# Windowed attention with a Swish feed-forward: wider loads, DMA transposes, an fp32 decay table, paired score tiles and an order fixed on three engines

## Chip, cores, metric

One core of one Trainium2 chip. The metric is the device time of one execution in microseconds (us). The profile adds a span (a few us shorter than the time) and the granted clock of the matmul engine. I write PE for TensorE, DVE for VectorE, ACT for ScalarE, POOL for GpSimd, and SP for the engine that issues loads.

## The reference

Batch 8, 8 heads, 576 tokens, head size 64. Each token attends to itself and the 127 before it, with an ALiBi bias; the result (4608 tokens x 512) goes through a feed-forward of width 2048 with a Swish of its own beta per column.

```python
scores = scale * np.matmul(q, k.transpose(0, 1, 3, 2))
rel = pos[:, None] - pos[None, :]
bias = slopes[:, None, None] * (-np.abs(rel))[None, :, :]
mask = (rel >= 0) & (rel < 128)
scores = np.where(mask, scores + bias[None], -1e9)
attn = softmax(scores)          # written out in the reference
x = (attn @ v) as (4608, 512)
h = x @ w_in
out = (h * (1.0 / (1.0 + np.exp(-beta * h)))) @ w_out
```

## The kernel before

The work of a batch is a list of steps: T (transpose q and k on PE), SC (scores sps, exp, mask, giving the probabilities pt), PV (pt times v gives pv, which DVE normalises into xn), X (transpose xn on PE into xt, and copy that into XT). They are packed between the steps of the feed-forward, HS (hps = W1 by XT) and OS (ops = gT by W2). Only PE's order is fixed by hand. First, the eight banks of PSUM, the memory in which this kernel's matmul results lie: two for hps, two for ops, one score tile of two banks, and two in `psum_t`, which pv and xt share. `merged(a, before)`: the pv steps of half a batch run among the scores of the next half.

```python
psum_h = ctx.enter_context(tc.tile_pool(name="psum_h", bufs=2, space=bass.MemoryType.PSUM))
psum_o = ctx.enter_context(tc.tile_pool(name="psum_o", bufs=2, space=bass.MemoryType.PSUM))
psum_s = ctx.enter_context(tc.tile_pool(name="psum_s", bufs=1, space=bass.MemoryType.PSUM))
psum_t = ctx.enter_context(tc.tile_pool(name="psum_t", bufs=2, space=bass.MemoryType.PSUM))
# ... (cut) in SC, after the score matmuls of one pair of heads:
for e in range(2):
    h = 2 * p + e
    for half, cols in ((0, slice(0, OWN[m])), (1, slice(OWN[m], 512))):
        nc.scalar.activation(out=pt[:, e, cols], in_=sps[:, e, cols], func=ACTF.Exp,
                             scale=qscale, bias=bias[:, half, h : h + 1])
nc.vector.tensor_tensor(out=pt[:], in0=pt[:], in1=masks[m][:], op=ALU.mult)   # bf16
# ... (cut) in PV, after the pv matmuls of four heads into one bank of psum_t:
nc.vector.reciprocal(out=zs[0:nq], in_=pv[0:nq, :, D : D + 1])
nc.vector.tensor_tensor(out=xn[0:nq, 4 * g : 4 * g + 4, :], in0=pv[0:nq, :, 0:D],
                        in1=zs[0:nq].broadcast_to([nq, 4, D]), op=ALU.mult)
# ... (cut) the order on PE:
for b in range(B):
    for m in range(2):
        a = [T(b, sb) for sb in ((0, 1, 2), (3, 4))[m]]         # shortened
        a += [SC(b, m, p) for p in range(NP)]                   # shortened
        att += merged(a, before)
        before = pvx(b, ((0, 1), (2, 3, 4))[m])
```

The softmax here doesn't subtract the row's maximum and nothing guards it: scores larger than these inputs give would overflow.

## Time and profile before

| | before |
|---|---|
| time, median of 2 runs | 376.41 us (375.89 to 376.93) |
| span, granted clock of the profiled run | 374.6 us, 0.9 or more in 39 of 40 slices |
| PE / DVE / ACT / POOL busy | 90 / 60 / 57 / 23% of the span |
| between 90 and 350 us: PE waiting for another engine | 0.6 us |

The lines behind this table stand in the prediction.

```profile
PE 80%; DMA 6%; DVE 4%; ACT 4%; SPq 4%; issue 1%; POOL 0%; ACTq 0%
```

Followed back from the last instruction, 80% of the time passes on PE and 4% on DVE.

### The profile page before, as it was taken

Reading aid. Unit: us, or ns where it says so; the run is one execution under the profiler, and the core shown is the slowest. Engines: PE = TensorE matmul, PEld = TensorE weight load, DVE = VectorE, ACT = ScalarE, POOL = GpSimd, SP = SyncE. Lnnn points to the kernel's source line nnn. Section 1 sums busy time; section 2 is a strip of 40 time slices with the busy share of each in tenths; the row PEclk is TensorE's granted clock in tenths of the full one; section 3 lists DMA queues with packets and bytes.
Section 4 is the critical chain, followed back from the end, with each engine's and each line's share of the span. In section 5 each row is a group of like instructions: output and inputs, shape, how many; then the busy total and the mean of one; then the engine's idle time right before and its main releaser. Section 6 shows DMA issues by size and latency. Waiting matters only on the chain.

```text
span 374.6 us, 6713 instructions
## 1 busy us (share of the span) xinstructions
PE 338.5 (90%) x2529; PEld 172.7 (46%) x2529; DVE 224.2 (60%) x473; ACT 214.4 (57%) x437; POOL 84.4 (23%) x151
## 2 busy tenths in 40 slices
PE   2367687788999999999999999999999999999995
PEld 1145334434454455445454545454545445544442
DVE  3266467777665677665666776776767755533400
ACT  1453359375745875585846694668566854445421
POOL 7570703453122213112033303320100000000000
PEclk9999999899999999999999999999999999999999
DMA  9999999999297898954138440000000010001012
GB/s 166 209 206 202 193 195 214 192 216 180 76 214 159 159 186 170 205 126 107 50 96 187 109 104 31 28 30 29 30 28 30 30 57 29 29 29 58 28 56 86
DMA packets 121985, 42.40 MB, mean 113 GB/s; under 512 B 113232, under 2 KB 117344, under 8 KB 121952
## 3 DMA queue, kind: packets, MB, share of 16 engines
q1 hardware_dynamic: 117728, 37.77, 47.9%
q0 software_dynamic: 4224, 4.19, 6.7%
q8 instruction: 20, 0.33, 0.4%
q14 instruction: 13, 0.11, 0.1%
HBM read 36.71 MB, written 9.44 MB: 123 GB/s over the span
## 4 chain that ended last, share of the span: by engine, by line
PE 80%; DMA 6%; DVE 4%; ACT 4%; SPq 4%; issue 1%; POOL 0%; ACTq 0%
PE ops L283 34%; PE hps L267 32%; PE sps L197 4%; DMA fst<-in_k_dram 4%; PE tps L171 4%; SPq L83 4%; ACT pt L207 3%; PE xt L249 2%; PE pv L233 2%; DVE gT L273 2%; PE pv L229 2%; DMA fst<-in_v_dram 1%; ACT sig L272 1%; DVE pt L211 1%; DVE qkT L176 1%
## 5 line engine op out<-in xcount | busy, mean ns | idle before, releaser
L272 ACT ACTIVATE sig<-hps,beta_h 128x512 bf16<-128x512 f32 x144 | 99.5, 692 | 98.4 <-PE hps L267 87.4
L267 PE MATMUL hps<-XT,W 128*128 128x512 bf16 x576 | 150.7, 385 | 3.6 <-DVE gT L273 3.0
L283 PE MATMUL ops<-W,gT 128*128 128x512 bf16 x576 | 144.9, 379 | 0.0
L273 DVE SCALAR_TENSOR_TENSOR gT<-sig,hps 128x512 bf16<-128x512 bf16 x144 | 98.3, 683 | 53.0 <-ACT sig L272 52.4
L207 ACT ACTIVATE pt<-sps,bias 128x256 bf16<-128x256 f32 (+2 forms) x256 | 100.4, 480 | 34.9 <-PE sps L197 34.6
L267 PEld LDWEIGHTS <-W 128*128 128x128 bf16 x576 | 51.1, 98 | 56.5 <-issue 10.9
L283 PEld LDWEIGHTS <-gT 128*128 128x128 bf16 x576 | 51.3, 98 | 52.2 <-issue 1.7
L211 DVE TENSOR_TENSOR pt<-pt,mask 128x1024 bf16<-128x1024 bf16 x64 | 46.1, 720 | 21.2 <-ACT pt L207 20.0
L96 POOL CAST bst<-fst 128x512 bf16<-128x512 f32 (+1 forms) x40 | 24.6, 615 | 108.8 <-issue 78.7
L197 PE MATMUL sps<-qkT 64*128 64x256 bf16 (+2 forms) x320 | 28.3, 271 | 14.1 <-ACT pt L207 13.1
L104 POOL CAST vs<-fst 128x512 bf16<-128x512 f32 (+1 forms) x40 | 26.1, 659 | 65.0 <-PE pv L233 38.1
L176 DVE COPY qkT<-tps 128x1024 bf16<-128x1024 bf16 (+1 forms) x40 | 25.5, 637 | 21.5 <-PE tps L171 21.3
L171 PE MATMUL tps<-ident,bst 128*128 128x128 bf16 x320 | 28.8, 240 | 7.8 <-POOL bst L96 4.3
L239 DVE TENSOR_TENSOR xn<-pv,zs 128x256 bf16<-128x256 f32 (+1 forms) x80 | 33.7, 422 | 2.6
L289 ACT ACTIVATE osb<-ops 128x512 f32<-128x512 f32 x36 | 21.6, 601 | 20.8 <-PE ops L283 20.8
L233 PE MATMUL pv<-vs,pt 128*128 128x65 bf16 x320 | 31.0, 200 | 2.5 <-DVE xn L239 1.5
L171 PEld LDWEIGHTS <-bst 128*128 128x128 bf16 x320 | 23.5, 107 | 17.3 <-POOL bst L96 4.9
L197 PEld LDWEIGHTS <-qkT 64*128 64x128 bf16 x320 | 12.4, 97 | 38.2 <-issue 35.1
L233 PEld LDWEIGHTS <-pt 128*128 128x128 bf16 x320 | 23.6, 102 | 13.7 <-issue 1.8
L97 POOL CAST bst<-fst 128x512 bf16<-128x512 f32 (+1 forms) x40 | 25.3, 634 | 9.3 <-DMA fst<-in_k_dram 9.2
L229 PE MATMUL pv<-vs,pt 128*128 128x65 bf16 x256 | 25.8, 200 | 1.8 <-DVE qkT L176 1.2
L229 PEld LDWEIGHTS <-pt 128*128 128x128 bf16 x256 | 21.3, 102 | 8.3 <-DVE xn L239 1.3
(26 smaller groups left out, 74.3 us busy)
## 6 DMA issues: line engine op xcount, KB each, us to landing
out_dram<-osb SPq DMA_DIRECT2D x36, 256.0 KB, 2.0
fst<-in_q_dram SPq DMA_DIRECT2D x32, 256.0 KB, 4.8
fst<-in_k_dram SPq DMA_DIRECT2D x32, 256.0 KB, 4.8
fst<-in_v_dram SPq DMA_DIRECT2D x32, 256.0 KB, 5.0
W<-in_moe_w_in_dram POOLq DMA_DIRECT2D x4, 512.0 KB, 11.5
W<-in_moe_w_out_dram POOLq DMA_DIRECT2D x4, 512.0 KB, 12.6
fst<-in_q_dram SPq DMA_DIRECT2D x8, 128.0 KB, 4.2
fst<-in_k_dram SPq DMA_DIRECT2D x8, 128.0 KB, 4.2
```

The lines of the kernel that those rows point to most:

```text
L171: nc.tensor.transpose(out=tps[:, i, p, :], in_=src[:, i, 2 * p : 2 * p + 2, :].rearrange("r h d -> r (h d)"), identity=ident[:],)
L176: nc.vector.tensor_copy(out=QK[b % 2][:, :, :, P * sb : P * sb + rows], in_=tps[:, :, :, 0:rows])
L197: nc.tensor.matmul(o, lhsT=qk[64 * e : 64 * e + 64, 1, p, P * kb : P * kb + P], rhs=qk[64 * e : 64 * e + 64, 0, p, P * kb : P * kb + nq], ...
L207: nc.scalar.activation(out=pt[:, e, cols], in_=sps[:, e, cols], func=ACTF.Exp, scale=qscale, bias=bias[:, half, h : h + 1],)
L211: nc.vector.tensor_tensor(out=pt[:], in0=pt[:], in1=masks[m][:], op=ALU.mult)
L229: nc.tensor.matmul(pv[:, hl, 0 : D + 1], lhsT=weights(b, qb - 1, h, 1), rhs=vs[:, qb - 1, h, 0 : D + 1], start=True, stop=False,)
L233: nc.tensor.matmul(pv[:, hl, 0 : D + 1], lhsT=weights(b, qb, h, 0), rhs=vs[:, qb, h, 0 : D + 1], start=qb == 0, stop=True,)
L239: nc.vector.tensor_tensor(out=xn[0:nq, 4 * g : 4 * g + 4, :], in0=pv[0:nq, :, 0:D], in1=zs[0:nq].broadcast_to([nq, 4, D]), op=ALU.mult,)
L267: nc.tensor.matmul(hps[:], lhsT=W1[:, c, bass.ts(j, P)], rhs=XT[:, c, c0 : c0 + TOKG], start=(c == 0), stop=(c == NDM - 1),)
L272: nc.scalar.activation(out=sig[:], in_=hps[:], func=ACTF.Tanh, scale=beta_h[:, j : j + 1])
L273: nc.vector.scalar_tensor_tensor(out=gts[g][:, j, :], in0=sig[:], scalar=1.0, in1=hps[:], op0=ALU.add, op1=ALU.mult)
L283: nc.tensor.matmul(ops_[:], lhsT=gT[:, j, i * P : i * P + P], rhs=W2[:, j, :], start=(j == 0), stop=(j == NFF - 1),)
```

## The change

The intent: let the loads run nearer line rate, take transposes off PE, make the exponentials fewer, and order all the issuing engines by hand.

1. Two tokens of q, k or v lie side by side on a partition, so that a row of a load has 512 B and not 256.
2. From batch 2 on, q and k are transposed by DMA (`DT`), from batch 3 on also the attention result (`X`), both issued by SP.
3. One exp per score tile without bias, into fp32; DVE multiplies it with an fp32 table that holds decay and mask.
4. Score tiles are made in pairs, which takes four PSUM banks; `psum_o` and `psum_t` give one each.
5. PE, SP and POOL in a fixed order (ACT and DVE too in the prologue).
6. Smaller: outputs issued by POOL in halves of 64 rows, v cast in quarters on POOL, 6 load buffers and not 16.

The diff, cut to its core (cuts are marked with `...`):

```diff
-    psum_o = ctx.enter_context(tc.tile_pool(name="psum_o", bufs=2, space=bass.MemoryType.PSUM))
-    psum_s = ctx.enter_context(tc.tile_pool(name="psum_s", bufs=1, space=bass.MemoryType.PSUM))
-    psum_t = ctx.enter_context(tc.tile_pool(name="psum_t", bufs=2, space=bass.MemoryType.PSUM))
+    psum_s = ctx.enter_context(tc.tile_pool(name="psum_s", bufs=2, space=bass.MemoryType.PSUM))
+    psum_o = ctx.enter_context(tc.tile_pool(name="psum_o", bufs=1, space=bass.MemoryType.PSUM))
+    psum_t = ctx.enter_context(tc.tile_pool(name="psum_t", bufs=1, space=bass.MemoryType.PSUM))
 ...
+    decay = const.tile([P, H, 3 * P], F32, name="decay")
 ...
+                r.append(nc.sync.dma_start(
+                    out=f[:, h0:h1].rearrange("p h c d -> p h (c d)"),
+                    in_=src[b, h0:h1, 256 * u : 256 * u + 256, :].rearrange(
+                        "h (p c) d -> p h (c d)", c=2),
+                ))
 ...
+                    nc.sync.dma_start(
+                        out=qk[:, :, at : at + 64],
+                        in_=src[64 * half : 64 * half + 64, c].rearrange("p i f -> p (i f)"),
+                        transpose=True,
+                    )
 ...
+            ex = ex_pool.tile([P, 2, 512], F32, name="ex", tag="ex")
+            nc.scalar.activation(
+                out=ex[:, :, 0:w], in_=sps[:, :, 0:w], func=ACTF.Exp, scale=qscale)
+            pt = pt_pool.tile([P, 2, 512], BF16, name="pt", tag="pt")
+            if m == 0:
+                nc.vector.tensor_tensor(
+                    out=pt[:, :, 0:w], in0=ex[:, :, 0:w], in1=decay[:, 2 * p : 2 * p + 2, :],
+                    op=ALU.mult)
 ...
+            for r0, r1, at in cuts:
+                nc.sync.dma_start(
+                    out=XT[:, :, at : at + r1 - r0], in_=xnv[r0:r1], transpose=True)
 ...
+            head = [A(0, 1), A(2, 3), pv(0, 0), pv(1, 0), Bm(0, 1), pv(0, 1), x(0), pv(1, 1),
+                    x(1), Bm(2, 3), pv(2, 0), pv(3, 0), C, pv(2, 1), x(2), pv(3, 1), x(3)]
+            tail = [pv(4, 0), pv(4, 1), x(4)]
 ...
+    with tc.manual_schedule(engines={ENG.PE, ENG.SP, ENG.Pool}):
```

`A(0, 1)` is the pair of score tiles 0 and 1 of the first half batch, `Bm` of the second, `C` the tile of the last 64 tokens, `pv(qb, g)` block qb of queries for head group g.

## The prediction

> **What bounds the kernel now.** I read the page's slices first, then the groups of instructions, then the timeline of the matmul engine (PE), then the DMA view of single stretches.
>
> ```profile
> PE   2367687788999999999999999999999999999995
> DVE  3266467777665677665666776776767755533400
> DMA  9999999999297898954138440000000010001012
> GB/s 166 209 206 202 193 195 214 192 216 180 76 214 159 159 186 170 205 126 107 50 96 187 109 104 31 28 30 29 30 28 30 30 57 29 29 29 58 28 56 86
> ```
>
> One slice is 374.6/40 = 9.4 us. There are two regimes: up to about 90 us DMA is saturated and PE is at 0.2 to 0.8; from 100 us PE is at 0.9 or more and DMA empties. So a gain can come from two places: fewer bytes-in-waiting early, and less PE work late. Where the early one ends:
>
> ```profile
> 42.44 1.87 PE L267 MATMUL hps<-XT,W 128*128 128x512 bf16 x4 [0.52 <-DVE XT L254]
> 80.19 1.89 PE L267 MATMUL hps<-XT,W 128*128 128x512 bf16 x8 [0.73 <-DVE gT L273]
> ```
>
> The first line is the first feed-forward matmul: 42 us pass before one can run. Counting hps matmuls in stretches of 5 us, 66 are done at 80 us, so token group 0 (64 of them) ends there: 42 to 80 us for 13.8 us of its own matmuls. What PE work costs is read from distances between starts in a stretch where PE never waits:
>
> ```profile
> 241.91 0.19 PE L229 MATMUL pv<-vs,pt 128*128 128x65 bf16 x1
> 242.16 1.03 PE L267 MATMUL hps<-XT,W 128*128 128x512 bf16 x4
> 243.11 0.39 PE L197 MATMUL sps<-qkT 64*128 64x256 bf16 x4
> 243.44 1.04 PE L283 MATMUL ops<-W,gT 128*128 128x512 bf16 x4
> 244.31 0.39 PE L249 MATMUL xt<-ident,xn 128*128 128x128 bf16 x4
> 244.53 1.03 PE L267 MATMUL hps<-XT,W 128*128 128x512 bf16 x4
> 248.64 0.61 PE L171 MATMUL tps<-ident,bst 128*128 128x128 bf16 x8
> 249.09 1.03 PE L267 MATMUL hps<-XT,W 128*128 128x512 bf16 x4
> ```
>
> Four 512-column matmuls take 244.31 - 243.44 = 0.87 us (0.216 each); eight transposes 0.45; four 0.22; eight pv matmuls 0.25; a score tile 0.33, and the four hps before it take 0.95 where 0.87 is usual, so 0.42 with the change of array shape. Per batch: T 5 x 0.45 = 2.25, X 5 x 0.22 = 1.1, scores 8 x 0.42 = 3.4, pv 72 x 0.031 = 2.25, together 9.0 us; 8 batches 72 us. Feed-forward: 1152 x 0.216 = 249 us. Sum 321 us; the span is 374.6, so 54 us are lost. After 80 us there remain 9/10 or so of the feed-forward (235 us) and 6.2 batches (56 us), 291 of the 294.6 us there: **almost all of the loss, some 50 us, lies before 80 us, and later PE alone sets the time.**
>
> **What the Trainium skill says.** (1) "DMA: Bandwidth & Descriptors", Specifications, gives 512 B or more as the least transfer for line rate. The trace agrees that 256 B is slow: between 3 and 12 us nothing but q, k, v moves, at 227 GB/s on average, whereas the weights in 24 to 34 us are written at
>
> ```profile
> q0 software_dynamic: 1644, 1.64, 97.1%
> ```
>
> 1.64 MB bf16, read as twice that in fp32, in 97% of 10 us: 340 GB/s read. (2) "VectorE: DVE Perf Modes", The TRN2 errata section, has (N+151)/0.96 ns for an fp32 add of two tensors, while bf16 pairs go at double rate. The present bf16 mask multiply of 1024 elements takes 690 ns on the timeline, (512+151)/0.96 = 691: agrees; no fp32 case is in this trace. (3) "ScalarE: Activation LUTs", What ACT_TABLE_LOAD costs, has 186 + 0.833 N ns with immediate operands. osb (N = 512): 612 against 601 in the groups; agrees. (4) The VectorE page, The three transpose paths, has 1309 ns for a 128x128 DMA transpose; no run here shows one.
>
> ```profile
> L289 ACT ACTIVATE osb<-ops 128x512 f32<-128x512 f32 x36 | 21.6, 601 | 20.8 <-PE ops L283 20.8
> L207 ACT ACTIVATE pt<-sps,bias 128x256 bf16<-128x256 f32 (+2 forms) x256 | 100.4, 480 | 34.9 <-PE sps L197 34.6
> L211 DVE TENSOR_TENSOR pt<-pt,mask 128x1024 bf16<-128x1024 bf16 x64 | 46.1, 720 | 21.2 <-ACT pt L207 20.0
> L171 PE MATMUL tps<-ident,bst 128*128 128x128 bf16 x320 | 28.8, 240 | 7.8 <-POOL bst L96 4.3
> L249 PE MATMUL xt<-ident,xn 128*128 128x128 bf16 x160 | 16.7, 231 | 0.0
> ```
>
> **The change, part by part.**
>
> *Rows of 512 B.* 256 B at 227 GB/s over 16 engines are 18 ns a row. If an engine's share of 435 GB/s gives 9.4 ns for the bytes, 9 ns are fixed; 512 B would then take 28 ns, 290 GB/s (an estimate from the page's fabric figure and the trace). The first group now waits for 512 tokens of q, k, v (3.1 MB, 11 us, landed near 14 us) and a first quarter of W1, not for 7.7 MB. What then bounds is batch 0's own chain: DVE has 4 x 0.96 + 4 x 1.22 us of multiplies, 4 copies of 0.69, 8 normalisations of 0.6, 4 copies of 0.42, some 18 us, starting near 7 us, and the scalar engine builds the decay table first. **First hps near 28 us instead of 42.**
>
> *Group 0* runs 9 HS alone (about 1.3 us each, bounded by the two hps banks, as two HS took 82.71 - 80.19 = 2.5 us before), then packs batch 1's attention into 7 HS. DVE there has 26 us. 12 + 26 to 28 gives 38 to 40 us, the 38 of before. End of group 0 near 66 to 68 us instead of 80: **-13 us.**
>
> *Transposes off PE.* T stays for batches 0 and 1, X for 0 to 2: PE loses 6 x 2.25 + 5 x 1.1 = 19 us, nearly all after 80 us, where PE is the bound: full worth. They become about 54 + 27 DMA transposes of 128 KB, issued a batch ahead, while the DMA row is at 0 to 4 from slice 18 on; hidden unless one takes over some 3 us. With the weights gone this leaves 36 us a batch for 12 us of loads and 9 to 14 transposes.
>
> *Scores in pairs.* Two tiles share one change of shape. The e = 0 and e = 1 matmuls run side by side (four of 256 took 0.33, not 0.43), so a first pair is 2 x (0.108 + 0.054) + 0.2 = 0.52, a second 0.63, the tail tile 0.44: 2.75 us a batch against 3.4. **-5 us.** PE work in all 321 - 19 - 5 = 297 us.
>
> *One exp per tile, fp32 table.* ACT: 768 and 1024 elements by the formula less the observed 10 ns, 0.82 and 1.03 us, per batch 4 x 0.82 + 5 x 1.03 = 8.4 us, against 100.4/8 = 12.6. DVE: 4 x 0.96 + 5 x 1.22 = 9.9 us a batch against 5.8, +33 us in all, against which 19 us of qkT copies and 10 us of XT copies go away. DVE stays near 228 us, but with a shorter span and its work shifted: in the late part per batch 9.9 + 10 x 0.6 + 18 x 0.68 = 28 of 36 us, 78%. Worth nothing directly, as neither engine is the bound there.
>
> *PSUM.* Score pairs take four banks, so ops and the shared bank for pv and xt fall from two buffers to one. A pv tile's bank comes free after about 0.2 + 0.18 + 0.42 + 0.2 = 1.0 us plus any wait for DVE, and an item between two pv is 0.87 us. Three or four pairs of pv a batch follow each other directly: 0.5 us each, about 2 us a batch. ops: 36 turns, an HS and a step between them (1.2 us) against 0.2 + 0.6 + the wait for ACT. I put both at **+14 us** in all (my choice in 5 to 25), and at the end three turns without an HS between them **+3 us**.
>
> *POOL.* Casts of v in quarter pieces and outputs issued there: about 12 us of casts and 9 issues of up to 0.8 us (the W issues took that) per batch, under 36 us.
>
> Sum: end of group 0 at 67, then 291 - 23 = 268 us of PE, stalls 14, end 3: 352 us. A fixed order worked out for three engines should pack group 0 better than I could and put the pv steps apart, so I take **343 us**.
>
> **Rivals.**
> 1. *PSUM and DVE become the bound.* The trace speaks for it a little: late in the run PE idle is 0 only because every bank had a second one. With 1.2 us multiplies in front of each gT and reciprocal the stall could be 1 us at each of 80 pv tiles and 36 ops turns: +50 instead of +14 us over 24 us gained on PE: 370 us or more, "same".
> 2. *DMA transposes are slow or hold up loads.* SP issues loads and transposes in one order, and a transpose waits for casts. If one takes 4 us, 14 x 4 + 12 = 68 us a batch against 36: the run becomes DMA bound late, 400 us and more. Against it: the DMA row shows free time for it, and two batches keep T on PE as if to cover the loaded start.
> 3. *No stall at all.* The order hides both: 62 + 268 + 3 = 333, or with a group 0 near 30 us long, 325 us.
>
> **Range and chances.** From 3 (325) to my sum with stalls at 25 (363): 322 to 362. Faster by over 2% means under 369: only a good part of rival 1 or 2 prevents it: 0.90; same 0.07; slower 0.03.
>
> **What would show it.** Right: first hps near 28 us; group 0 done at 62 to 68; DMA above 270 GB/s while q, k, v load; exp rows at 0.82 and 1.03 us, multiplies at 0.96 and 1.22; PE at 0.9 in late slices with idle in front of pv and ops of 10 to 20 us, released by DVE xn and ACT osb. Wrong: waits of sps for DMA (rival 2), hps waiting for gT late (rival 1), GB/s unchanged near 220, or POOL casts so delayed that transposes come late.

## The result, and the profile after

The changed kernel takes **421.69 us** (419.70 to 423.67, 2 runs), against 376.41. Every ratio below is the mean time of one kernel's fast runs over the mean of the kernel before's fast runs in the same rounds, so it isn't quite the ratio of the medians quoted. Here it is 1.121, 95% interval 1.108 to 1.134: 12% slower. The profiled run: span 417.7 us, granted clock 0.961.

From the page after: PE's busy tenths and its granted clock in 40 slices of 10.4 us, then the last chain by engine and by line.

```profile
PE   3448675679679788589948974799998999999984
PEclk9999969799899999899989998799999999999999
...
PE 51%; DVE 25%; ACT 9%; DMA 5%; issue 4%; SPq 3%; another core or an unknown queue 1%; POOL 1%; ACTq 0%
PE hps L399 22%; PE ops L416 21%; DVE pt L313 8%; ACT ex L302 6%; DVE pt L306 5%; DVE gT L405 5%; PE pv L360 4%; DMA XT<-xn 4%; DVE xn L366 3%; PE sps L282 2%; ACT sig L404 2%; SPq L264 2%; DVE qkT L243 1%; DMA fst<-in_k_dram 1%
```

The wall of nines that stood from slice 11 to the end now starts only at slice 27; before that PE falls to 4 and 5 again and again. PE's work did shrink (324.3 us busy against 338.5). DVE went from 4% of the chain to 25%, though its busy time hardly rose (232.1 us against 224.2) and its share of the span fell from 60% to 56%. The new multiplies (L313 and L306) alone are 13% of the chain, 54 us of 418. So DVE isn't full. It is *in the way*. What PE waited for in the whole span (total us, times, longest):

```profile
PE pv L360 <- DVE xn L366: 21.1, 18, 3.1
PE hps L399 <- DMA XT<-xn: 19.3, 5, 6.5
PE xt L380 <- DVE xn L366: 9.1, 7, 3.7
PE sps L282 <- DVE qkT L243: 8.4, 6, 2.5
```

And the new operations themselves, groups by form (busy us, then mean ns of one):

```profile
L313 DVE TENSOR_TENSOR pt<-ex,decay 128x1024 bf16<-128x1024 f32 x32 | 40.9, 1320 | 13.3 <-ACT ex L302 13.3
L306 DVE TENSOR_TENSOR pt<-ex,decay 128x768 bf16<-128x768 f32 x32 | 31.6, 1027 | 9.6 <-ACT ex L302 9.5
L302 ACT ACTIVATE ex<-sps 128x1024 f32<-128x1024 f32 x32 | 30.9, 1021 | 18.4 <-PE sps L282 18.4
```

How one wait of each of the two big kinds comes about is seen in the timeline after (start, us, engine, line, operation):

```profile
155.86 0.62 PE L282 MATMUL sps<-qkT 64*128 64x128 bf16 x12
...
157.28 0.41 PE L360 MATMUL pv<-vs,pt 128*128 128x65 bf16 x8
...
157.60 2.36 DVE L313 TENSOR_TENSOR pt<-ex,decay 128x1024 bf16<-128x1024 f32 x2 [0.22 <-ACT ex L302]
...
159.88 0.18 DVE L365 RECIPROCAL zs<-pv 128x4 f32<-128x4 f32 x1
...
160.54 0.42 DVE L366 TENSOR_TENSOR xn<-pv,zs 128x256 bf16<-128x256 f32 x1
...
161.02 0.42 PE L360 MATMUL pv<-vs,pt 128*128 128x65 bf16 x8 [1.60 <-DVE xn L366]
...
164.64 5.19 SPq L264 DMA_TRANSPOSE qkT<-bst  x4
...
165.32 0.42 DVE L366 TENSOR_TENSOR xn<-pv,zs 128x256 bf16<-128x256 f32 x1
...
169.94 1.27 SPq L386 DMA_TRANSPOSE XT<-xn  x1
...
174.18 1.87 PE L399 MATMUL hps<-XT,W 128*128 128x512 bf16 x4 [5.14 <-DMA XT<-xn]
```

The first six lines: a pair of score tiles at 155.86 leads to two multiplies back to back on DVE, 2.36 us. A pv that PE finished at 157.69 needs DVE for a reciprocal of 0.18 and a product of 0.42 us, but stands behind both (the product also behind one gT). It gives its bank back at 160.96, 3.3 us after PE was done with it. There is one such bank now, so the next pv waits, and in PE's fixed order everything behind it waits too. Neither pv needs these two multiplies: their own probabilities were multiplied at 150.37. In the whole list of PE's waits there is no line of pv for pt (there is one for pc, the probabilities of the last 64 tokens, 4.5 us).

The last four: xn is ready at 165.74, but SP has begun to issue four transposes of q and k for the next batch, 1.3 us each. The transpose of xn is issued at 169.94, and the next feed-forward matmul starts at 174.18, 8.4 us after xn. This wait comes from SP's order, not from a late xn. Then the four matmuls take 1.87 us where 1.03 is usual: the Trainium skill ("TensorE: Matmul & The Clock Gate", Part 1) says that PE falls to half rate after an idle window of some 3.4 us, and here PE had been idle for 5.14. The granted clock agrees: 0.91 between 160 and 180 us, 1.00 before and after. Waits here cost something twice.

### The profile page after: what moved, and what is told of

It is laid out like the page before. It is cut to its first block, busy times and chain, and to the rows that moved or that the text cites. A ratio compares the mean times of both kernels' runs of the same rounds, so it can differ in the third digit from the quotient of the medians.

```text
span 417.7 us, 6134 instructions
## 1 busy us (share of the span) xinstructions
PE 324.3 (78%) x2276; PEld 154.7 (37%) x2317; DVE 232.1 (56%) x413; ACT 187.7 (45%) x274; POOL 139.8 (33%) x212
## 4 chain that ended last, share of the span: by engine, by line
PE 51%; DVE 25%; ACT 9%; DMA 5%; issue 4%; SPq 3%; another core or an unknown queue 1%; POOL 1%; ACTq 0%
PE hps L399 22%; PE ops L416 21%; DVE pt L313 8%; ACT ex L302 6%; DVE pt L306 5%; DVE gT L405 5%; PE pv L360 4%; DMA XT<-xn 4%; DVE xn L366 3%; PE sps L282 2%; ACT sig L404 2%; SPq L264 2%; DVE qkT L243 1%; DMA fst<-in_k_dram 1%
## 5 line engine op out<-in xcount | busy, mean ns | idle before, releaser
L399 PE MATMUL hps<-XT,W 128*128 128x512 bf16 x559 | 153.2, 395 | 24.5 <-DMA XT<-xn 19.3
L432 POOL DMA_DIRECT2D out_dram<-osb x64 | 33.4, 527 | 199.8 <-ACT osb L422 199.8
L302 ACT ACTIVATE ex<-sps 128x768 f32<-128x768 f32 (+1 forms) x64 | 55.3, 915 | 29.9 <-PE sps L282 29.5
L313 DVE TENSOR_TENSOR pt<-ex,decay 128x1024 bf16<-128x1024 f32 x32 | 40.9, 1320 | 13.3 <-ACT ex L302 13.3
L204 POOL CAST vs<-fst 64x512 bf16<-64x512 f32 x60 | 44.9, 748 | 7.2 <-DMA fst<-in_v_dram 4.8
L192 POOL CAST bst<-fst 128x1024 bf16<-128x1024 f32 (+1 forms) x36 | 35.4, 1004 | 24.2 <-PE tps L239 9.1
L360 PE MATMUL pv<-vs,pt 128*128 128x65 bf16 x448 | 26.4, 204 | 20.3 <-DVE xn L366 15.6
L306 DVE TENSOR_TENSOR pt<-ex,decay 128x768 bf16<-128x768 f32 x32 | 31.6, 1027 | 9.6 <-ACT ex L302 9.5
L360 PEld LDWEIGHTS <-pt 128*128 128x128 bf16 x448 | 22.4, 105 | 37.9 <-DVE xn L366 23.0
L282 PE MATMUL sps<-qkT 64*128 64x128 bf16 (+1 forms) x320 | 20.7, 262 | 9.2 <-DVE qkT L243 8.4
L365 DVE RECIPROCAL zs<-pv 128x4 f32<-128x4 f32 (+1 forms) x80 | 14.1, 176 | 14.7 <-PE pv L360 14.7
```

Source lines behind the costliest of these rows:

```text
L192: return eng.tensor_copy(out=o, in_=f[:, h0:h1].rearrange("p h c d -> p c h d"))
L204: r = e.copy(out=o, in_=a) if e is nc.scalar else e.tensor_copy(out=o, in_=a)
L282: nc.tensor.matmul(o, lhsT=qk[64 * e : 64 * e + 64, 1, p, P * kb : P * kb + P], rhs=qk[64 * e : 64 * e + 64, 0, p, q0 : q0 + n], start=Tru ...
L302: nc.scalar.activation(out=ex[:, :, 0:w], in_=sps[:, :, 0:w], func=ACTF.Exp, scale=qscale)
L306: nc.vector.tensor_tensor(out=pt[:, :, 0:w], in0=ex[:, :, 0:w], in1=decay[:, 2 * p : 2 * p + 2, :], op=ALU.mult)
L313: nc.vector.tensor_tensor(out=pt[:].rearrange("p e (n w) -> p e n w", n=2), in0=ex[:].rearrange("p e (n w) -> p e n w", n=2), in1=d, op=AL ...
```

## The experiments

Three theories, after the first reading:

- **XT late.** The DMA transposes of X come late behind those of q and k in SP's order; put X back on PE and most of the loss goes.
- **Load.** The fp32 multiplies bring DVE to its limit; whatever the order, the time stays.
- **Placement.** PE's fixed order puts pv just behind scores, with one bank for pv and xt. A DVE instruction of 1.3 us is then on PE's path, while with more distance and two banks it would cost little. (I first took these scores to be pv's own; the lists show that they are not, see point 5 of the change.)

All ratios: below 1 is faster than the kernel before. The medians are of all 4 runs, the ratios of the fast ones alone: one run of `e1` and two of `e12` were slow.

**1. Undo one thing at a time** (before in these rounds: 375.18 us).

X back on PE:
```diff
-    PE_X = 3
+    PE_X = 8
```

> After, with the X transposes of all batches back on PE (PE_X 3 to 8), all else the same. Theory A (X by DMA arrives late, because the DMA transposes of X stand in the SP order behind four 1.26 us transposes of qkT and the loads): the 19.3 us that hps waits for DMA XT<-xn go, and with them most of the low-clock stretches after those stalls (granted clock 0.91, 0.91, 0.86 at 160, 200, 260 us, some 8 us); PE gets 25 X steps of 0.22 us back (5.5 us): about 421 - 27 + 6 = 400 us. Theory B (one bank for pv and xt, freed only after fp32 multiplies on DVE): the stalls of hps go but the X steps queue up for the same bank, each with a wait of up to 1 us for DVE: 415 us or no gain at all.

Measured: 425.93 us, 1.127 [1.118, 1.136]. No gain. The wait of hps for XT is gone from its waits, but xt waits for DVE xn 27.1 us now (9.1 in the change) and pv for xn 21.3. XT late is not the cause *by itself*: remove it and PE stands at the next place, at xt, which in PE's order follows directly behind the pv whose xn it needs.

Tables and exp tile in bf16:
```diff
-    decay = const.tile([P, H, 3 * P], F32, name="decay")
+    decay = const.tile([P, H, 3 * P], BF16, name="decay")
```
(and the same for `decayt` and `ex`)

> After, with ex and both decay tables in bf16, so that the multiply can run at double rate: 1024 elements in about 0.7 us for 1.32, 768 in about 0.55 for 1.03 (the old bf16 mask multiply of 1024 took 0.69). DVE loses some 36 of 83 us of multiplies. Theory B (pv waits for DVE xn, which stands behind pairs of multiplies): PE waits for DVE xn, pc and qkT (some 24 us late, 20 us early) fall by a third to a half: 400 to 410 us. Theory A alone: XT is late all the same, 415 to 420 us.

Measured: 383.51 us, 1.023 [1.018, 1.028]: 38 us, most of the loss. The multiplies fall to 743 and 621 ns. Waits of PE in this kernel:

```profile
PE hps L399 <- DMA XT<-xn: 15.1, 3, 5.7
PE pv L360 <- DVE xn L366: 6.9, 10, 1.9
```

That fits load *and* placement, as it makes the instruction both cheaper and quicker. It takes later runs to tell them apart.

PSUM divided as before the change, score tiles one at a time (pairs need four banks, so the two go together):
```diff
-  psum_s bufs=2   psum_o bufs=1   psum_t bufs=1      # shortened
+  psum_s bufs=1   psum_o bufs=2   psum_t bufs=2
-        A = lambda *ps: (None, lambda: SC(b, 0, ps))
+        A = lambda *ps: (None, [(None, lambda p=p: SC(b, 0, (p,))) for p in ps])
```

> After, with the PSUM banks shared out as before (score tiles 1 of two banks, ops 2, pv and xt 2) and score tiles one by one, each a step of its own, everything else as after. Theory B: PE waits for DVE xn (21 us for pv, 9 for xt) and for ACT osb (4) mostly go, 0.1 us a score tile comes back for changes of shape (6 us): 395 to 405 us. If pairs of score tiles matter more than banks: 420 us or more. Theory A: hps still waits about 19 us for XT.

Measured: 401.84 us, 1.070 [1.065, 1.076]: 20 us back. The wait of pv for xn is gone, that of hps for XT stays, and those of xt for xn and of sps for the exp have grown (9.1 and 0.7 us in the change):

```profile
PE hps L403 <- DMA XT<-xn: 18.6, 3, 7.2
PE xt L384 <- DVE xn L370: 11.1, 11, 2.4
PE sps L282 <- ACT ex L306: 10.6, 20, 1.2
```

Rows of 256 B, two DMAs where the change has one:
```diff
-                    in_=src[b, h0:h1, 256 * u : 256 * u + 256, :].rearrange(
-                        "h (p c) d -> p h (c d)", c=2),
+                        in_=src[b, h0:h1, 256 * u : 256 * u + 256, :].rearrange(
+                            "h (p c) d -> p c h d", c=2)[:, c],     # for c in range(2)
```

> After, with q, k and v fetched in rows of 256 B again (one DMA for even and one for odd rows; same places in memory), all else the same. q, k, v then move at about 220 GB/s instead of 286 in the first 10 us: first hps some 4 to 5 us later; group 0 to 2 some 5 to 10 us later, nothing later on unless the DMA transposes collide with loads: 427 to 435 us. If the loads are hidden (rival): 421 us.

Measured: 424.34 us, 1.131 [1.126, 1.136]. The 512 B rows are worth about 1% here, which is within the noise. They do run faster: between 3 and 10 us the changed kernel moves 286 GB/s, this run 222. But the first hps comes at 36.4 us here and at 35.6 in the change.

**2. Combinations** (before: 375.29). I put pv half a batch behind its scores, as it was before the change (`e6`, and `e8` with bf16 and X on PE). Both gave **wrong results**, relative error 0.10: the loads of the next batch cast v into a buffer that pv of two batches back still had to read. An order is also a claim on buffers; the later pv needs a third buffer for v. I draw nothing from their times (432.67 and 395.47 us).

> After, fp32 table and all, with one thing changed in PE's order for batches 2 to 7: the pv and X steps of a half batch stand beside the score steps of the next half, as in the kernel before, and not one or two items behind their own score steps. Theory C (the fp32 multiplies hurt as latency: PE's fixed order puts pv so close behind its scores that exp, two multiplies and the bank's release lie on PE's path): PE waits for DVE fall by more than half, and most of what bf16 gave (38 us) comes back: 385 to 400 us. Theory D (the fp32 multiplies hurt as load: DVE has too much to do in each group): no gain, 412 to 425 us.

> bf16 tables, X on PE and the later pv order together. If distance and length of the multiplies are the same wait (theory C), the order adds little to bf16: within 5 us of the bf16 version with X on PE. If DVE load matters beside it, 8 us or more.

`e7` joins the edits of `e1` and `e3` (`PE_X = 8`, bf16 tables and exp tile), `e9` those of `e1`, `e3` and `e4`:

> The bf16 version with all X transposes on PE as well. The bf16 version alone took 383 us and still has 15.1 us in which hps waits for DMA XT<-xn, in 3 stalls, and 0.97 mean clock. Theory A in its weaker form (late XT is real, but with fp32 multiplies in front the X steps on PE waited just as long for DVE): now X on PE should pay: 383 - 15 - 5 for the clock + 6 for 100 transposes, 368 to 374 us. If X on PE still gains nothing, the waiting is for xn itself: 380 to 388 us.

> bf16 tables, X on PE, and the banks of before (score tiles singly in 1 buffer, ops 2, pv and xt 2). On the fp32 version the banks gave 20 us. If that was the wait for pv's bank behind fp32 multiplies, bf16 has taken most of it and 0 to 5 us are left, against 5 us for changes of shape and waits of sps for exp: 366 to 376 us. If the banks act on their own, 355 to 362 us.

Measured: `e7` 375.95 us, 1.002 [0.996, 1.008]; `e9` 381.20 us, 1.015 [1.007, 1.022]. Once the multiplies are short, X on PE is worth 2% where it was worth nothing in `e1`, and the second bank with single tiles alone is worth nothing (1.3 points worse). The parts don't add; each hides behind another.

**3. Distance with three v buffers** (before: 376.36). The edit, shortened: the head and tail lists of batches 2 and on are replaced by

```python
head = merged(scores_of_first_half,  pv_and_x_of_last_second_half) \
     + merged(scores_of_second_half, pv_and_x_of_own_first_half)
VS = [... for i in range(3)]     # and to make room: ptp 9, osb 3, sig 2 buffers
```

The order alone, all else as in the change (fp32, one bank, X by DMA):

> The earlier try of this order was wrong in its result and of no use: v of batch b+1 was cast into the buffer that pv of batch b-1 still read. Here v has three buffers (ptp 9, osb 3, sig 2 to make room); the order of pv one half batch behind the scores, fp32 table kept. Theory C (latency of exp, multiplies and bank between a score step and its pv): 385 to 400 us. Theory D (DVE load): no gain, 412 to 430 us.

Measured: 408.89 us, 1.077 [1.067, 1.088], so 4 points better than the change. Its profiled run was slow, so of its waits I take only the kinds:

```profile
PE pv L361 <- DVE xn L367: 28.1, 15, 3.1
PE hps L400 <- DMA XT<-xn: 2.5, 1, 2.5
```

pv still waits for its bank, hps for XT hardly. This is the opposite of `e4`, where the banks took away the first wait and left the second. The result fell between load and placement, and settled nothing between these two.

Order with bf16 and X on PE, one bank; then with two banks and single tiles ("the repaired kernel"; its lists place the single tiles and X a little differently, see 5); then bf16 with q and k, not X, transposed on PE:
```diff
-    PE_T = 2
+    PE_T = 8        # and DT returns at once for these batches
```

> The same order with three v buffers, bf16 tables and X on PE; without the order it took 376 us. Theory C: 365 to 378 us, the order and bf16 heal the same wait. If one bank for pv and xt is now the wait, it stays at 370 to 380 us.

> All the repairs at once, so near the kernel before in its attention: banks of before, score tiles singly, pv half a batch behind, X one or two steps behind its pv, bf16 tables, X on PE; kept of the change: 512 B rows, T by DMA, one exp a tile, the fixed order. PE work is then 249 + 8 x (3.4 + 2.25 + 1.1) + 4.5, some 307 us, and first hps at 36 us. If the order and the banks are what is left: 340 to 355 us, faster than both. If the early part still decides: 362 to 370 us.

> bf16 tables, all T on PE, X of batches 3 to 7 still by DMA: no transposes of qkT stand in front of XT in the SP order. Theory A (queue): hps waits for DMA XT fall from 15.1 us to under 5 us. If it is the transpose's own 2.7 us to landing: they stay at 10 us or more. PE gets 6 x 2.25 = 13.5 us of T, and T uses the one bank: 385 to 397 us in all.

Measured: `e13` 379.48 us, 1.009 [1.004, 1.014]. `e15` **366.73 us, 0.975 [0.969, 0.980]**, the first to beat the kernel before. Order alone (1.009 against 1.002 of `e7`) and banks alone (1.015) each gave nothing to this version, both together almost 3 points. `e14` 398.83 us, 1.059 [1.052, 1.066]: without the q and k transposes in SP's order the wait for XT is gone, so it was the queue; but pv now waits 11.3 us for the copies of q and k on DVE, as their tile shares the one bank.

**4. The split between the theories** (before: 374.70). In the repaired kernel I put single parts of the change back.

fp32 again, and its control: bf16 with the same smaller buffers that fp32 needs to fit.
```diff
-    decay = const.tile([P, H, 3 * P], BF16, name="decay")     # decayt and ex too
+    decay = const.tile([P, H, 3 * P], F32, name="decay")
-  ptp bufs=10   osb bufs=4   sig bufs=3      # shortened; e19 has these three alone
+  ptp bufs=9    osb bufs=3   sig bufs=2
```

> The repaired kernel (366.7 us) with the fp32 decay table, fp32 exp tile and fp32 multiply put back, nothing else but one buffer fewer of three small tiles so that it fits. Latency theory (the long multiplies only hurt because they stand just in front of the pv matmuls and of the one pv and xt bank): with pv half a batch later and two banks it stays within 2% of the repaired kernel, 366 to 374 us, multiplies still at 1.03 and 1.32 us. Load theory (27 us more work on DVE overfill it, whatever the order): 385 to 410 us, with waits of pv and xt for DVE xn of 15 us or more.

> Control for the fp32 run: the repaired kernel, still in bf16, with the same smaller numbers of buffers for pt, osb and sig (9, 3, 2). Expected within 1% of the repaired kernel, 365 to 371 us; if it is 375 or more, the fp32 run can't be read as the cost of fp32.

Measured: `e16` 372.81 us, 0.995 [0.988, 1.001]; control `e19` 365.77 us, 0.974 [0.969, 0.979]. fp32 costs **2.1 points, 7 us**, where it cost 38 us in the change. The groups of `e16` by form: L318, the 1024-element multiply, has a median of 1225 ns, the 1226 ns of the change. Same instructions, same number, a fifth of the cost. With X on PE on both sides, as here, the change's order and bank make fp32 dearer still: `e7` to `e1` is 12.5 points, about 50 us. The load theory is out as the main cause.

X by DMA again (`PE_X = 3` instead of 8), and 256 B rows (the edit of `e5`):

> The repaired kernel with X of batches 3 and on made by DMA transposes on SP's queue, as in the change. If the wait of hps for XT seen after the change (19 us) comes from SP's order and not from the slow multiplies, it is here again at 10 us or more and the time is 374 to 385 us. If it came from xn being late behind the multiplies, it stays under 4 us and the time is 361 to 368 us, as PE does 5 us less work.

> The repaired kernel with q, k and v read in 256 B rows, two DMAs where there was one. In the change itself the rows were worth at most 1% because the early stretch waited for DVE and ACT. If the early stretch of the repaired kernel is bound by the same chain, 367 to 372 us; if the 512 B rows are what it lives on, first hps several us later and 376 us or more.

Measured: `e17` **360.18 us, 0.960 [0.950, 0.969]**, best of all; the wait for XT doesn't come back, so the DMA transposes of X are a gain of some 1.4 points (5 to 6 us) in the repaired kernel. This is small: the intervals touch, and two of the four runs of `e17` had a clock of 0.995 (358 us), two of 0.981 (362 us), where the control at 0.979 to 0.984 took 365 to 366. `e18` 365.37 us, 0.972 [0.967, 0.978]: no loss from 256 B rows here either. PE's busy tenths and the last chain in `e17`:

```profile
PE   1555865768999999999999999999999999999994
...
PE 81%; DVE 9%; ACT 5%; issue 2%; DMA 1%; SPq 0%; POOL 0%; ACTq 0%
```

**5. The missing corner** (before: 374.83). Order and banks put back together: the buffers of `e12`, the bank edit of `e4`, and the lists of `e15`. These are not quite the lists of `e12`: single score tiles are spread among the pv steps, the pv of one block follow each other, and X stands 3 to 6 steps behind its last pv, where in `e12` and in the change it follows directly. Nothing else is undone: fp32, X and T by DMA, 512 B rows and the fixing of three engines all stay.

> The change as it is (fp32 table, fp32 multiply, X and T by DMA, 512 B rows) with only the place of pv (half a batch behind its scores, X one or two steps later, three v buffers) and the PSUM division (two pv and xt banks, two ops banks, two single-pair score buffers) put back. Placement theory: order and banks together give back what neither gave alone (order alone 408.9, banks alone 401.8), 360 to 372 us, waits of hps for XT under 5 us. Load theory, or SP's order: 380 us or more, with pv waiting for DVE xn or hps for XT 10 us or more.

Measured: **368.46 us, 0.981 [0.976, 0.987]**. Its waits of PE between 81 and 330 us, the largest three:

```profile
PE pv L365 <- DVE pc L337: 1.3, 1, 1.3
PE hps L404 <- DVE gT L410: 1.0, 2, 0.6
PE xt L385 <- DVE xn L371: 0.6, 1, 0.6
```

Its multiplies are no faster than in the change (means of 1260 and 1188 ns, against 1320 and 1027), its DVE does as much (235.7 us), and DVE is down from 25% to 11% of the last chain. PE waits for other engines and DMAs 3.8 us between 85 and 330 us, where the changed kernel waits 44.9.

The four corners, with everything else as in the change:

| | one bank, score pairs | two banks, single tiles |
|---|---|---|
| order of the change | 1.121 (the change) | 1.070 |
| pv half a batch behind | 1.077 (lists of `e12`) | **0.981** (lists of `e15`) |

The corners are from different rounds, each against the kernel before on its own chip. Banks alone give 5 points, order alone 4, both together 14. Each repair takes away one of the two big waits: the banks that of pv for xn, the order that of hps for XT. With one of them the other wait remains; only with both can DVE be late without PE noticing. What the runs don't separate: the second bank from the single tiles, as pairs need the banks; and, within the order, the place of pv from those of X and of SP's transposes, which move along with it. How much of the 14 points is due to the better lists of `e15` isn't shown either. In the kernels with two banks the waits point to X: what the order takes away there is hps for XT (18.6 us in `e4`, none in `e20`) or, with X on PE, xt for xn (7.7 us after 85 us in `e9`, none in `e15`).

## Why the prediction was wrong

It said 343 us, in 322 to 362. Step by step:

- **What bounds the kernel before: right**, PE alone after the start; its late waits are 0.6 us.
- **The step that failed: PSUM, "+14 us in all (my choice in 5 to 25)"**, and beside it the DMA transposes, "hidden unless one takes over some 3 us". After 80 us the prediction had 268 us of PE work and 17 us of stalls (14 + 3). In the changed kernel PE is busy for 280 us there (the clock is 0.97) and idle for 58; in the kernel before it is busy 288 and idle 6, in the run with order and banks put back 277 and 9. Of the waits after 81 us, 26 us are of the kind that the PSUM term was to cover (pv for xn 17.0, xt for xn 5.1, ops for osb 4.2), almost double (xt may also wait for xn as its input); 19.3 us are hps for XT, which the sum had at nothing.
- *The bank.* It was to come free "after about 1.0 us plus any wait for DVE", and that wait was set to nothing. Tile by tile in the records of the trace (62 pv tiles after 85 us), the time from the last matmul to the end of the product has a median of 1.03 us, as predicted, but a mean of 1.7; 22 take over 2 us, the longest 4.5. In the kernel before the median is 0.7 and none takes over 1.6. In `e20` DVE is no quicker (median 1.7, mean 1.6), but PE waits for it 0.5 us in all after 85 us. So the delay stayed, and its cost went.
- *The transposes of X.* They land 2.7 us after issue in the median, within what the prediction allowed. It had them "issued a batch ahead", which held for q and k only: X can't be issued before xn is there, and then stood in SP's queue.
- *What undid it.* The run with order and banks put back moves the ratio from 1.121 to 0.981, some 53 us: the whole loss and a little gain. It differs from the changed kernel in the lists, the banks with single tiles, and the buffers that these take.
- **"Worth nothing directly, as neither engine is the bound there"**, said of the one exp and the fp32 table, is the same error seen from the other side. 78% (or the 56% of the page) is a load. What counted was the time in front of the reciprocal. With the order of the change and one bank fp32 costs 38 us, with the far order and two banks 7. The durations were right: medians of 958 and 1226 ns against 957 and 1224, exps at 809 and 1021 against 820 and 1030.
- **"A fixed order ... should ... put the pv steps apart"** was a hope, and the diff said the contrary: the lists have pv(0, 0) and pv(1, 0) in a row directly behind the pair A(2, 3), whose multiplies then stand before their reciprocals, where `merged` spread the pv steps among transposes and single score tiles. I had both before me and didn't compare them.
- **Rival 1** (PSUM and DVE become the bound) **was right in its mechanism** and too small, at "370 us or more". Its sum is wrong: by the prediction's own terms a stall of 50 gives 67 + 268 + 50 + 3 = 388 us, and 1 us at each of 80 + 36 turns is 116 us, not 50. It also left out the wait for XT and the clock. Its sign, hps waiting for gT late, didn't come (1.5 us between 85 and 330 us).
- **Rival 2** (DMA transposes hold up) was right in part: SP takes 1.2 to 1.3 us to issue each, and X stood behind four of q and k. It shows as 19.3 us of waits, but undoing it alone gave nothing (`e1`), and in the far order it hardly occurs (2.5 us in `e12`, none in `e20` and `e17`).
- **Rows of 512 B: rate right (286 GB/s against 290), worth wrong.** The first hps came at 35.6 us, not 28, and token group 0 ends at about 80 us in both kernels, where 13 us of gain were predicted. In both places where rows were undone nothing was lost beyond 1%: in the change the chain that ended last runs up to 35 us through batch 0's own transposes, scores, exps and multiplies (the latter 2.2 to 2.8 us a pair). That part the prediction had named, and took too short.
- **Transposes off PE: right, once it can be seen.** The part for X (5 batches of 1.1 us) measured 5 to 6 us between `e19` and `e17` (about 4 at an equal clock), which differ also in three buffer counts; these alone gave nothing (0.974 against 0.975 of `e15`).
- **Score pairs: unseen.** -5 us of PE work needs four banks, and every version that beats the kernel before gave the pairs up.

Open: what the single parts of the order edit give; what single parts of point 6 of the change do (POOL's casts and outputs, fewer load buffers), which no run undid; and why `e17` is still 17 us over the prediction. Part of that is the start: its group 0 ends at 72 us, 5 later than predicted, and PE's busy tenths are at 5 to 8 up to about there.

## What to carry to other kernels

An engine at 56% can still set the time: when another engine runs in a fixed order, ask for each instruction what stands before its reader in the reader's queue and how many banks lie between, and compare that in both kernels before counting any busy time. Make a slow step cheap by order and buffers before making it fast: here the order and the second bank with single tiles did more (53 us) than halving the multiply (38 us), and either repair alone, the order in a somewhat different form, gave about a third of it. A part of a change that seems worthless when undone alone may be hidden behind another (X by DMA: nothing, then a cost of 2%, then a gain of 1.4 points), so test it in the version that no longer stalls.

## What the Trainium skill lacked or had wrong

- "DMA: Bandwidth & Descriptors", DMA Transpose (X-bar): that section has no time for the issue of a transpose. Here a DMA transpose of 64x1024 bf16 held SP for 1.19 us at least, 1.26 in the median, and landed 2.8 us after issue; a queue of four is 5.2 us in front of whatever comes next on SP. "VectorE: DVE Perf Modes", The three transpose paths, has 1309 ns for 128x128; from issue to landing the larger transposes of X (up to 128x512) took 2.3 us at the least and 2.7 in the median. No run here has the page's size.
- "VectorE: DVE Perf Modes", The TRN2 errata: (N+151)/0.96 gives 957 and 1224 ns for the fp32 multiplies, and the medians are 958 and 1226. But the mean is 7 to 8% higher (1027 and 1320), and the formula has no term for what POOL does meanwhile. In the trace of the change 13 of the 64 multiplies take over 3% more than the median of their form (up to 2.06 us); 12 of these begin while a cast of POOL is running, and only 5 of the other 51 do. In `e20` all 16 long ones do, and 8 of the other 48. That the casts hold them up is a reading of this coincidence; no run tested it.
- No page that I read gives a time for how long a PSUM bank stays taken behind the queue of the engine that reads it: 3.3 us in the case shown here, for 0.6 us of reading.
